# A decode step of attention and gated MLP: wo loaded behind the last V, V as the moving operand of PV, gate/up summed c-major, and wq loaded in two partition blocks

## The chip, the cores and the metric

One core of one Trainium2 chip. The metric is the device time of one execution in microseconds (us), lower is better. Each experiment is timed beside runs of the kernel before on the same chip. A "ratio" is the mean time of one kernel's fast runs over the mean of the other's fast runs of the same rounds, so it is not quite the ratio of the medians that are quoted. The profile shows one execution. Its span is about 2 us shorter than the time.

Names used by the profile: PE is the matmul engine and PEld its weight loads, DVE, ACT and POOL are the vector, scalar and GpSimd engines, SP is the engine that issues most loads. A load "lands" when its completion is signalled. SBUF is the memory on the chip that the loads write; its tiles span up to 128 partitions on the page (128x4096). The "granted clock" is the share of full speed that PE was allowed. PV is the product of the softmax weights p with V. In gate and up, m counts the 14 blocks of output columns (13 of 128, the last of 64) and c the 5 blocks of 128 input rows: "m-major" finishes one m before the next, "c-major" one c.

## The reference, cut to what matters

```python
# x: 1 token of 640; 32 heads of 128; K and V caches 32 x 4096 x 128, bf16
h  = x + attention(layernorm(x), k_cache, v_cache, wq, wo)
h2 = h + (gelu(ln(h) @ w_gate) * (ln(h) @ w_up)) @ w_down      # 640 -> 1728 -> 640
# attention: q = ln(x) @ wq; p = softmax(q . k / sqrt(128)); o = p @ v; o @ wo
```

K and V are 64 MiB (16 loads of 4 MiB, four heads each), wq and wo 5 MiB each, the MLP weights 6.3 MiB. Every byte is used once, so this is a kernel of loads.

## The kernel before

All large loads go through one queue (SP), in the order wq, K0, K1, V0, K2, V1, ..., K7, V6, wo (part), V7, wo (rest), w_gate, w_up, w_down. Three slots of SBUF hold K and V. Scores are made by a DVE product, an identity matmul that folds it, and a DVE sum. The parts that the argument touches:

```python
# wq: two column blocks, each over all 128 partitions
wq_v = A_wq[:, :].rearrange("(p c) n -> p c n", c=5)
d_wq = [P.dma("sync", wq_sb[:, 0:2, :], wq_v[:, 0:2, :]),
        P.dma("sync", wq_sb[:, 2:5, :], wq_v[:, 2:5, :])]
...
# before the last V: wo's first half and half of the second
if n == len(order) - 1:
    wo_load("0", 0, 0, 16)
    wo_load("1a", 1, 0, 8)
...
# PV: V is the weight (128 columns), p moves (4 columns); 128 of these for each group of heads
i = e.matmul(po[:, o:o + 4], vt[:, g, :], p_bd[:, G % 2, g, :], start=(g == 0), stop=(g == 127))
...
# gate and up: m-major, columns 13 apart (w_down's rows are blocked to match)
for m in range(14):
    for c in range(5):
        ws = w[:, c, m:1664:13] if m < 13 else w[:, c, 1664:1728]
        i = e.matmul(ps[0:k, m:m + 1], ws, hlnT[:, c:c + 1], start=(c == 0), stop=(c == 4))
```

The softmax here doesn't subtract the row's maximum and nothing guards it: scores larger than these inputs give would overflow.

## Time and profile before

208.41 us, median of 4 runs (208.35 to 208.57).

| of the profile before | us |
|---|---|
| span | 206.4 |
| first product of K0 starts (K0 has landed) | 25.7 |
| last V has landed | 182.9 |
| gate and up, 140 matmuls | 192.6 to 201.4 |
| last load (w_down) has landed | 202.1 |
| last matmul ends | 204.1 |

No compute engine is busy for even two thirds of the span, and the DMA row is 9 nearly throughout, so the loads set the pace.

The end of the chain of waits of the kernel before (start us, duration us, what):

```profile
182.96 1.88 PE bank L287 x64
...
192.57 8.81 PE bank L377 x140
201.38 0.64 PE bank L386 x8
202.02 2.09 PE bank L405 x37
204.11 0.02 issue
204.14 0.31 DVE out_row L412
```

From the landing of the last V on, the chain is compute: PV (L287), a projection and a layernorm (left out), gate and up (L377), the residual, w_down's product (L405).

### The profile page before, as it was taken

The page shows a single profiled execution, that of the slowest core. Times are in us where ns is not written, and L with a number is a line of the kernel's source. Part 1 is how long each engine was busy: PE and PEld are TensorE (multiplying, and loading weights), DVE is VectorE, ACT ScalarE, POOL GpSimd, SP SyncE. Part 2 cuts the span into 40 slices and gives each one's busy share as a digit, 9 for nine tenths or more (in the row PEclk, how much of TensorE's full clock was granted, in tenths as well). Part 3 has the DMA queues.
Part 4 walks back from the last instruction along what each step waited for, and adds up shares of the span by engine and source line. Part 5 has one row for each costly group of instructions (what it writes and reads, how often), then busy time and mean ns, then how long its engine had stood idle before and what let it go on. Part 6 is the DMA issues. An engine that isn't in the chain of part 4 may idle for free.

```text
span 206.4 us, 3919 instructions
## 1 busy us (share of the span) xinstructions
PE 128.2 (62%) x1715; PEld 75.2 (36%) x1715; DVE 100.3 (49%) x103; ACT 56.4 (27%) x265; POOL 3.8 (2%) x10
## 2 busy tenths in 40 slices
PE   1205058486987909671877488469818596348795
PEld 1101023132722703260327124423613186337693
DVE  3001088779479247816772877079437920000221
ACT  3001004606606602540353036205600560000101
POOL 7000000000000000000000000000000000000000
PEclk9999658969958967995797579757976985555555
DMA  6999999999999999999999999999999999999970
GB/s 219 445 448 419 464 438 407 426 467 427 413 403 470 432 416 407 470 429 419 402 470 422 426 403 465 426 422 407 464 429 426 413 403 433 421 435 429 372 285 6
DMA packets 3844, 84.47 MB, mean 409 GB/s; under 512 B 434, under 2 KB 500, under 8 KB 628
## 3 DMA queue, kind: packets, MB, share of 16 engines
q1 hardware_dynamic: 3826, 84.23, 95.8%
q8 instruction: 13, 0.21, 0.4%
q14 instruction: 3, 0.02, 0.0%
q10 hardware_dynamic: 2, 0.00, 0.0%
HBM read 84.23 MB, written 0.00 MB: 408 GB/s over the span
## 4 chain that ended last, share of the span: by engine, by line
DMA 57%; PE 24%; DVE 15%; issue 2%; SPq 1%; ACT 0%; DVEq 0%
DMA slot<-in_A_k_cache_dram 41%; DMA slot<-in_A_v_cache_dram 16%; DVE prod L251 12%; PE bank L259 10%; PE bank L287 6%; PE bank L377 4%; DVE sc L266 2%; PE bank L319 2%; PE bank L405 1%; SPq L51 1%; PE bank L386 0%; PE bank L215 0%; PE bank L298 0%; PE bank L310 0%; DVEq L419 0%
## 5 line engine op out<-in xcount | busy, mean ns | idle before, releaser
L259 PE MATMUL bank<-prod,id_b 128*128 128x512 bf16 x256 | 75.2, 454 | 50.7 <-DVE prod L251 50.7
L251 DVE TENSOR_TENSOR prod<-slot,qb 128x4096 bf16<-128x4096 bf16 x32 | 72.4, 2285 | 28.5 <-DMA slot<-in_A_k_cache_dram 28.5
L270 ACT ACTIVATE p_bd<-sc,zero_t 32x32 bf16<-32x32 f32 x128 | 46.4, 362 | 97.2 <-DVE sc L266 96.0
L259 PEld LDWEIGHTS bank<-prod,id_b 128*128 128x128 bf16 x256 | 26.9, 113 | 96.9 <-DVE prod L251 60.5
L266 DVE TENSOR_REDUCE sc<-bank 128x32 f32<-128x512 f32 x32 | 22.0, 688 | 22.3 <-PE bank L259 22.3
L287 PE MATMUL bank<-p_bd,slot 128*128 128x4 bf16 x1024 | 27.5, 165 | 6.3 <-DMA slot<-in_A_v_cache_dram 6.3
L287 PEld LDWEIGHTS bank<-p_bd,slot 128*128 128x128 bf16 x1024 | 27.4, 98 | 7.9 <-DMA slot<-in_A_v_cache_dram 3.3
L270 ACT ACTIVATION_READ_ACCUMULATOR p_bd<-sc,zero_t 32x1 f32 x128 | 23.5, 184 | 0.0
L235 PE MATMUL bank<-arena,xlnB 128*32 128x512 bf16 x40 | 4.6, 628 | 10.0 <-DMA arena<-in_A_wq_dram 10.0
L377 PE MATMUL bank<-hlnT,slot 128*128 128x1 bf16 (+1 forms) x140 | 8.8, 199 | 1.5 <-DVE hlnT L365 1.5
L377 PEld LDWEIGHTS bank<-hlnT,slot 128*128 128x128 bf16 (+1 forms) x140 | 8.7, 165 | 1.7 <-DVE hlnT L365 1.6
L303 DVE TENSOR_TENSOR attnN<-bank,rz 128x16 bf16<-128x16 f32 x2 | 0.3, 174 | 17.4 <-PE bank L287 17.4
L319 PE MATMUL bank<-aP,arena 128*128 128x1 bf16 x160 | 7.0, 179 | 1.6 <-issue 1.2
L319 PEld LDWEIGHTS bank<-aP,arena 128*128 128x128 bf16 x160 | 6.9, 132 | 1.8 <-issue 1.5
L219 ACT ACTIVATE ln<-ln,eps_t 128x1 f32<-128x1 f32 x2 | 0.6, 294 | 24.5 <-DVE ln L217 24.5
L241 DVE CAST qb<-bank 128x512 bf16<-128x512 f32 x1 | 0.7, 692 | 13.1 <-PE bank L235 13.1
L235 PEld LDWEIGHTS bank<-arena,xlnB 128*32 128x32 bf16 x40 | 1.3, 133 | 12.5 <-issue 6.3
L242 ACT CAST qb<-bank 128x512 bf16<-128x512 f32 x1 | 0.6, 585 | 13.6 <-PE bank L235 13.6
L414 ACT CAST out_row<-bank 1x160 bf16<-1x160 f32 x2 | 0.6, 285 | 6.0 <-PE bank L405 5.9
L405 PE MATMUL bank<-slot,hm 128*1 128x160 bf16 (+1 forms) x56 | 2.1, 331 | 0.0
L390 DVE COPY g_t<-bank 128x14 f32<-128x14 f32 x1 | 0.2, 173 | 3.8 <-PE bank L377 3.8
L364 DVE TENSOR_TENSOR hT<-xx,bank 128x5 f32<-128x5 f32 x1 | 0.2, 161 | 3.7 <-PE bank L319 3.7
(55 smaller groups left out, 23.1 us busy)
## 6 DMA issues: line engine op xcount, KB each, us to landing
slot<-in_A_k_cache_dram SPq DMA_DIRECT2D x8, 4096.0 KB, 22.1
slot<-in_A_v_cache_dram SPq DMA_DIRECT2D x7, 4096.0 KB, 17.5
slot<-in_A_v_cache_dram SPq DMA_DIRECT2D x2, 2048.0 KB, 29.6
arena<-in_A_wq_dram SPq DMA_DIRECT2D x1, 3072.0 KB, 14.7
arena<-in_A_wo_dram SPq DMA_DIRECT2D x1, 2560.0 KB, 23.1
arena<-in_A_wo_dram SPq DMA_DIRECT2D x2, 1280.0 KB, 30.6
slot<-in_B_w_gate_dram SPq DMA_DIRECT2D x1, 2160.0 KB, 26.5
slot<-in_B_w_up_dram SPq DMA_DIRECT2D x1, 2160.0 KB, 31.9
```

The lines of the kernel that those rows point to most:

```text
L51: ev = self.op(eng, lambda e: e.dma_start(out, in_), *deps, dma=True)
L219: l3 = A(lambda e: e.activation(ln[:, 3:4], ln[:, 2:3], ACTF.Ln, bias=eps_t[:, 0:1], scale=-1.0), l2, c_eps)
L235: i = e.matmul(ps_q[hf][32 * j:32 * j + 32, :], xlnB[:, c, :], wq_j[:, c, j, 4 * hf:4 * hf + 4, :], start=(c == 0), stop=(c == 4))
L241: qa = V(lambda e: e.tensor_copy(qb[:, 0:4, :].rearrange("p g d -> p (g d)"), ps_q[0][:, :]), qd)
L251: m = V(lambda e: e.tensor_tensor(out=prod[:, s % 4, :, :], in0=kt[:, 32 * u:32 * u + 32, :], in1=qb[:, G, :].unsqueeze(1).to_broadcast([1 ...
L259: i = e.matmul(ps_f[s % 2][:, :], id_b[:, :], prod[:, s % 4, :, 16 * b:16 * b + 16], start=(b == 0), stop=(b == 7))
L266: reds[s] = V(lambda e: e.reduce_sum(sc[:, s % 4, :], ps_f[s % 2][:, :].rearrange("p (g d) -> p g d", d=16), axis=AX.X), folds[s], exps.ge ...
L270: x = A(lambda e, j=j: e.activation(p_bd[32 * j:32 * j + 32, G % 2, 32 * (s % 4):32 * (s % 4) + 32, j], sc[32 * j:32 * j + 32, s % 4, :], ...
L287: i = e.matmul(po[:, o:o + 4], vt[:, g, :], p_bd[:, G % 2, g, :], start=(g == 0), stop=(g == 127))
L319: r = e.matmul(ps_p[:, c:c + 1], wo_sb[:, t, i, c::5], aP[:, t, i:i + 1], start=(t == 0 and c == 0 and i == 0), stop=(t == 1 and i == 15), ...
L377: i = e.matmul(ps[0:k, m:m + 1], ws, hlnT[:, c:c + 1], start=(c == 0), stop=(c == 4))
L405: i = e.matmul(ps_d[32 * q:32 * q + 1, 0:160], hm[0:k, m:m + 1], wd_sb[0:k, m, 160 * q:160 * q + 160], start=False, stop=(last and m == ms ...
```

## The change

Its intent, as we read the diff: take PV and the projection off the tail by loading all of wo behind the last V; make PV cheaper with V as the moving operand; make gate/up start on what has landed; and start the stream of loads sooner with a first load of 16 rows, one for each of the 16 DMA engines that the page counts. The diff, cut to its core:

```diff
-    wq_v = A_wq[:, :].rearrange("(p c) n -> p c n", c=5)
-    d_wq = [P.dma("sync", wq_sb[:, 0:2, :], wq_v[:, 0:2, :]),
-            P.dma("sync", wq_sb[:, 2:5, :], wq_v[:, 2:5, :])]
+    wq_v = A_wq[:, :].rearrange("(p c) n -> p (c n)", c=5)
+    d_wq = [P.dma("sync", arena[0:16, :], wq_v[0:16, :]),
+            P.dma("sync", arena[16:128, :], wq_v[16:128, :])]
 ...
-            if n == len(order) - 1:
-                wo_load("0", 0, 0, 16)
-                wo_load("1a", 1, 0, 8)
 ...   # PV: 32 matmuls for each group, p as weights of 16 columns, on four column tiles
-                    i = e.matmul(po[:, o:o + 4], vt[:, g, :], p_bd[:, G % 2, g, :], ...)
+                for b in range(32 // parts * k, 32 // parts * (k + 1)):
+                    a = 32 * (b % 4)
+                    i = e.matmul(po[a:a + 16, :], p_bd[:, G % 2, 4 * b:4 * b + 4, :].rearrange("p g j -> p (g j)"),
+                                 vt[:, 4 * b:4 * b + 4, :], start=(b < 4), stop=(b >= 28))
+        evs[G] = A(lambda e: e.copy(po_sb[:, G % 2, :], po[:, :]), pvs[G], ...)   # then 4 fp32 matmuls pick the heads
 ...
+    wo_load("0", 0, 0, 16)          # all behind the last V
+    wo_load("1a", 1, 0, 12)
+    wo_load("1b", 1, 12, 16)
 ...   # w_up in 3 + 2 of its 5 c blocks; w_down in rows 12, 13, then 8 + 2 + 2
-            for m in range(14):
-                for c in range(5):
-                    ws = w[:, c, m:1664:13] if m < 13 else w[:, c, 1664:1728]
+            for c in cs:
+                for m in range(14):
+                    ws = w[:, c, 512 * (m // 4) + m % 4:512 * (m // 4) + 512:4] if m < 12 else \
+                        w[:, c, 128 * m:min(128 * m + 128, DF)]
```

The q projection, which ran two of its five column blocks before the rest of wq had landed, now waits for both loads.

More of the change, by code (lines that the diff above doesn't have):

```diff
@@ L22 @@
 NSLOT = 3
-WD1 = 11
 class Ev:
@@ L111, in bass_sequential_preLN__gqa_block_cached__glu_gated_geglu__decode_kernel @@
     hlnT = sb("hlnT", [128, 5], BF16)
-    rz = sb("rz", [128, H], FP32)
-    attnN = sb("attnN", [128, H], BF16)
+    rz = sb("rz", [16, 2], FP32)
+    po_sb = sb("po_sb", [128, 2, 512], FP32)
+    hs_t = sb("hs_t", [128, 4, 16], FP32)
+    hs = sb("hs", [128, 4, 28], FP32)
     aT = sb("aT", [16, 2, 128], BF16)
@@ L133, in bass_sequential_preLN__gqa_block_cached__glu_gated_geglu__decode_kernel @@
     ps_g, ps_u = bank[0], bank[1]
-    ps_q = [bank[3], bank[4]]
-    ps_d = bank[3]
+    ps_q = [bank[3], bank[7]]
+    ps_a = bank[3]
+    ps_d = bank[3][:, 256:416]
     ps_o = [bank[2], bank[4]]
@@ L139, in bass_sequential_preLN__gqa_block_cached__glu_gated_geglu__decode_kernel @@
     ps_p = bank[7]
-    wq_sb = arena[:, :].rearrange("p (c n) -> p c n", c=5)
     wo_sb = arena[:, :].rearrange("p (t i n) -> p t i n", t=2, i=16)
@@ L201, in bass_sequential_preLN__gqa_block_cached__glu_gated_geglu__decode_kernel @@
                                          fill=0.0, base=0, channel_multiplier=-8), c_onesb)
+    GP(lambda e: e.memset(hs[:, :, :], 0.0))
+    c_hs = GP(lambda e: e.affine_select(hs_t[:, :, :], ones_f[:, 0:64].rearrange("p (a b) -> p a b", a=4),
+                                        pattern=[[-32, 4], [-1, 16]], compare_op=ALU.is_equal,
+                                        fill=0.0, base=0, channel_multiplier=1), c_ones)
     c_pbd = GP(lambda e: e.memset(p_bd[:, :, :, :], 0.0))
     c_rs = GP(lambda e: e.memset(RS[:, :, :], 0.0))
+    c_po = [V(lambda e, b=b: e.memset(bank[b][:, :], 0.0)) for b in (2, 4)]
+    c_hs = V(lambda e: e.reduce_sum(hs[:, :, 12:16], hs_t[:, :, :].rearrange("p t (g j) -> p g j t", g=4), axis=AX.X), c_hs)
     def x_cols(e):
@@ L228, in bass_sequential_preLN__gqa_block_cached__glu_gated_geglu__decode_kernel, with q_proj @@
     wq_j = arena[:, :].rearrange("p (c g j d) -> p c j g d", c=5, g=NG, j=4)
-    def q_part(cs):
-        def fn(e):
-            for c in cs:
-                for hf in range(2):
-                    for j in range(4):
-                        i = e.matmul(ps_q[hf][32 * j:32 * j + 32, :], xlnB[:, c, :],
-                                     wq_j[:, c, j, 4 * hf:4 * hf + 4, :], start=(c == 0), stop=(c == 4))
-            return i
-        return fn
-    T(q_part([0, 1]), xl, d_wq[0])
-    qd = T(q_part([2, 3, 4]), d_wq[1])
+    def q_proj(e):
+        for c in range(5):
+            for hf in range(2):
+                for j in range(4):
+                    i = e.matmul(ps_q[hf][32 * j:32 * j + 32, :], xlnB[:, c, :],
+                                 wq_j[:, c, j, 4 * hf:4 * hf + 4, :], start=(c == 0), stop=(c == 4))
+        return i
+    qd = T(q_proj, xl, *d_wq)
     qa = V(lambda e: e.tensor_copy(qb[:, 0:4, :].rearrange("p g d -> p (g d)"), ps_q[0][:, :]), qd)
     qc = A(lambda e: e.copy(qb[:, 4:8, :].rearrange("p g d -> p (g d)"), ps_q[1][:, :]), qd)
-    folds, reds, exps, pvs = {}, {}, {}, {}
+    folds, reds, exps, pvs, evs, hds = {}, {}, {}, {}, {}, {}
     def score_mult(s):
@@ L280, in pv_group @@
         vt = view(n)
-        po = ps_o[G // 4]
-        o = 4 * (G % 4)
+        po = ps_o[G % 2]
         parts = len(landed[n])
@@ L285, in pv @@
             def pv(e, k=k):
-                for g in range(128 // parts * k, 128 // parts * (k + 1)):
-                    i = e.matmul(po[:, o:o + 4], vt[:, g, :], p_bd[:, G % 2, g, :],
-                                 start=(g == 0), stop=(g == 127))
-                return i
-            pvs[G] = consumed[n] = T(pv, exps[4 * G + 3], landed[n][k], qc)
+                for b in range(32 // parts * k, 32 // parts * (k + 1)):
+                    a = 32 * (b % 4)
+                    i = e.matmul(po[a:a + 16, :], p_bd[:, G % 2, 4 * b:4 * b + 4, :].rearrange("p g j -> p (g j)"),
+                                 vt[:, 4 * b:4 * b + 4, :], start=(b < 4), stop=(b >= 28))
@@ new lines, in pv, with head_sum @@
+                return i
+            pvs[G] = consumed[n] = T(pv, exps[4 * G + 3], landed[n][k], evs.get(G - 2), *c_po)
+        evs[G] = A(lambda e: e.copy(po_sb[:, G % 2, :], po[:, :]), pvs[G], hds.get(G - 2))
+        def head_sum(e):
+            g = G % 4
+            for r in range(4):
+                i = e.matmul(ps_a[0:16, 128 * (G // 4):128 * (G // 4) + 128], hs[:, r, 12 - 4 * g:28 - 4 * g],
+                             po_sb[:, G % 2, 128 * r:128 * r + 128], start=(g == 0 and r == 0), stop=(g == 3 and r == 3))
+            return i
@@ L293, in bass_sequential_preLN__gqa_block_cached__glu_gated_geglu__decode_kernel @@
+        return head_sum
     zs = {}
     def sum_half(t):
-        hs = slice(16 * t, 16 * t + 16)
-        r = V(lambda e: e.reduce_sum(RT[:, hs], RS[:, hs, :], axis=AX.X), exps[16 * t + 15])
-        z = T(lambda e: e.matmul(ps_z[:, 0:16], ones_f[:, :], RT[:, hs], start=True, stop=True), r)
-        zs[t] = V(lambda e: e.reciprocal(rz[:, hs], ps_z[:, 0:16]), z)
+        hh = slice(16 * t, 16 * t + 16)
+        r = V(lambda e: e.reduce_sum(RT[:, hh], RS[:, hh, :], axis=AX.X), exps[16 * t + 15])
@@ L301, in finish_half @@
+        z = T(lambda e: e.matmul(ps_z[0:16, 0:1], RT[:, hh], ones_f[:, 0:1], start=True, stop=True), r)
+        zs[t] = V(lambda e: e.reciprocal(rz[:, t:t + 1], ps_z[0:16, 0:1]), z)
     def finish_half(t):
-        hs = slice(16 * t, 16 * t + 16)
-        z2 = V(lambda e: e.tensor_mul(attnN[:, hs], ps_o[t][:, 0:16], rz[:, hs]), zs[t], pvs[4 * t + 3])
-        ps_t = ps_z[0:16, 64:128].bitcast(BF16)
-        z3 = T(lambda e: e.transpose(ps_t, attnN[:, hs], id_b[:, :]), z2)
-        z4 = V(lambda e: e.tensor_copy(aT[:, t, :], ps_t), z3)
+        z4 = V(lambda e: e.tensor_scalar(aT[:, t, :], ps_a[0:16, 128 * t:128 * t + 128], rz[:, t:t + 1], None, ALU.mult),
+               zs[t], hds[4 * t + 3])
@@ L313, in finish_half, with proj_part @@
         return V(lambda e: e.tensor_copy(aP[:, t, :], ps_z[:, 32:48]), z5)
-    def proj_half(t, ev, *ws):
+    def proj_part(t, lo, hi, *ws):
         def fn(e):
             for c in range(5):
-                for i in range(16):
+                for i in range(lo, hi):
                     r = e.matmul(ps_p[:, c:c + 1], wo_sb[:, t, i, c::5], aP[:, t, i:i + 1],
@@ L322, in fn @@
             return r
-        return T(fn, ev, *ws)
+        return T(fn, *ws)
     def scores(G):
@@ L333, in bass_sequential_preLN__gqa_block_cached__glu_gated_geglu__decode_kernel @@
     scores(0)
+    heads = None
     for G in range(NG):
@@ L336, in bass_sequential_preLN__gqa_block_cached__glu_gated_geglu__decode_kernel @@
             scores(G + 1)
-        if G == 3:
-            sum_half(0)
-        if G == NG - 1:
-            sum_half(1)
-            proj_half(0, a0, d_wo["0"])
-        pv_group(G)
-        issue(pos[("V", G)] + 1 + NSLOT)
-        if G == 3:
-            a0 = finish_half(0)
-    wo_load("1b", 1, 8, 16)
-    sl = [slots[(len(order) + i) % NSLOT] for i in range(2)]
+        if G in (3, NG - 1):
+            sum_half(G // 4)
+        if heads is not None:
+            hds[G - 1] = T(heads, evs[G - 1], c_hs, qa, qc)
@@ L350, in bass_sequential_preLN__gqa_block_cached__glu_gated_geglu__decode_kernel @@
+        if G == 4:
+            a0 = finish_half(0)
+        heads = pv_group(G)
+        issue(pos[("V", G)] + 1 + NSLOT)
+    hds[NG - 1] = T(heads, evs[NG - 1])
+    a1 = finish_half(1)
+    wo_load("0", 0, 0, 16)
+    wo_load("1a", 1, 0, 12)
+    wo_load("1b", 1, 12, 16)
+    sl = [slots[(len(order) + i) % NSLOT] for i in range(1, 3)]
+    free = [consumed[len(order) - NSLOT + i] for i in range(1, 3)]
     wg_sb = sl[0][:, 0:5 * DF].rearrange("p (c n) -> p c n", c=5)
     wu_sb = sl[0][:, 5 * DF:10 * DF].rearrange("p (c n) -> p c n", c=5)
-    wd_sb = sl[1][:, 0:14 * D].rearrange("p (c n) -> p c n", c=14)
@@ L353, in bass_sequential_preLN__gqa_block_cached__glu_gated_geglu__decode_kernel @@
-    wd_v = B_w_down[0:1664, :].rearrange("(p c) n -> p c n", c=13)
-    d_wg = P.dma("sync", wg_sb, B_w_gate[:, :].rearrange("(p c) n -> p c n", c=5), consumed[len(order) - NSLOT])
-    d_wu = P.dma("sync", wu_sb, B_w_up[:, :].rearrange("(p c) n -> p c n", c=5))
-    d_wd = [P.dma("sync", wd_sb[0:64, 13, :], B_w_down[1664:1728, :], consumed[len(order) - NSLOT + 1]),
-            P.dma("sync", wd_sb[:, 0:WD1, :], wd_v[:, 0:WD1, :]),
-            P.dma("sync", wd_sb[:, WD1:13, :], wd_v[:, WD1:13, :])]
+    wd_sb = sl[1][:, 0:14 * D].rearrange("p (m n) -> p m n", m=14)
@@ new lines, in bass_sequential_preLN__gqa_block_cached__glu_gated_geglu__decode_kernel @@
+    wu_v = B_w_up[:, :].rearrange("(p c) n -> p c n", c=5)
+    wd_v = B_w_down[0:1536, :].rearrange("(a p r) n -> p a r n", a=3, r=4)
+    wd_d = wd_sb[:, 0:12, :].rearrange("p (a r) n -> p a r n", a=3)
+    d_wd = [P.dma("sync", wd_sb[:, 12, :], B_w_down[1536:1664, :], free[1]),
+            P.dma("sync", wd_sb[0:64, 13, :], B_w_down[1664:1728, :])]
+    d_wg = P.dma("sync", wg_sb, B_w_gate[:, :].rearrange("(p c) n -> p c n", c=5), free[0])
+    d_wu = [P.dma("sync", wu_sb[:, 0:3, :], wu_v[:, 0:3, :]),
+            P.dma("sync", wu_sb[:, 3:5, :], wu_v[:, 3:5, :])]
@@ L360, in bass_sequential_preLN__gqa_block_cached__glu_gated_geglu__decode_kernel @@
+    d_wd += [P.dma("sync", wd_d[:, 0:2, :, :], wd_v[:, 0:2, :, :]),
+             P.dma("sync", wd_d[:, 2, 0:2, :], wd_v[:, 2, 0:2, :]),
+             P.dma("sync", wd_d[:, 2, 2:4, :], wd_v[:, 2, 2:4, :])]
     V(lambda e: e.memset(ps_g[64:128, 13:14], 0.0), reds[31])
     V(lambda e: e.memset(ps_u[64:128, 13:14], 0.0), reds[31])
-    a1 = finish_half(1)
-    pr = proj_half(1, a1, d_wo["1a"], d_wo["1b"])
+    proj_part(0, 0, 16, a0, d_wo["0"])
+    proj_part(1, 0, 12, a1, d_wo["1a"])
+    pr = proj_part(1, 12, 16, d_wo["1b"])
@@ L368, in bass_sequential_preLN__gqa_block_cached__glu_gated_geglu__decode_kernel, with glu @@
                                      in1=hT[:, 0:5].unsqueeze(1).to_broadcast([128, 128, 5]), op=ALU.mult), h, c_idf)
-    def glu(ps, w):
+    def glu(ps, w, cs):
         def fn(e):
-            for m in range(14):
-                k = 128 if m < 13 else 64
-                for c in range(5):
-                    ws = w[:, c, m:1664:13] if m < 13 else w[:, c, 1664:1728]
-                    i = e.matmul(ps[0:k, m:m + 1], ws, hlnT[:, c:c + 1], start=(c == 0), stop=(c == 4))
-            return i
-        return fn
-    ga = T(glu(ps_g, wg_sb), hl, d_wg)
-    up = T(glu(ps_u, wu_sb), d_wu)
+            for c in cs:
+                for m in range(14):
+                    ws = w[:, c, 512 * (m // 4) + m % 4:512 * (m // 4) + 512:4] if m < 12 else \
+                        w[:, c, 128 * m:min(128 * m + 128, DF)]
+                    k = 128 if m < 13 else 64
+                    i = e.matmul(ps[0:k, m:m + 1], ws, hlnT[:, c:c + 1], start=(c == 0 and m == 0), stop=(c == 4),
+                                 skip_group_check=True)
+            return i
+        return fn
+    ga = T(glu(ps_g, wg_sb, range(5)), hl, d_wg)
     def resid(e):
@@ L388, in resid @@
         return i
-    T(resid, hx, qa)
+    T(resid, hx)
+    T(glu(ps_u, wu_sb, range(3)), d_wu[0])
+    up = T(glu(ps_u, wu_sb, range(3, 5)), d_wu[1])
     g1 = V(lambda e: e.tensor_copy(g_t[:, :], ps_g[:, 0:14]), ga)
@@ L409, in down @@
         return fn
-    T(down([13] + list(range(WD1)), False), g9, d_wd[0], d_wd[1])
-    dn = T(down(list(range(WD1, 13)), True), d_wd[2])
+    T(down([12, 13], False), g9, d_wd[0], d_wd[1])
+    T(down(range(8), False), d_wd[2])
+    T(down([8, 9], False), d_wd[3])
+    dn = T(down([10, 11], True), d_wd[4])
     os = [V(lambda e, q=q: e.tensor_copy(out_row[0:1, 160 * q:160 * q + 160], ps_d[32 * q:32 * q + 1, 0:160]), dn)
```

## The prediction

The forecast came to 206.4 us, 2.0 below the 208.41 before: 1.7 from the tail, which leaves 0.3 for the start (how the start was weighed is not stated). The start was also on the critical path, with a gain of up to 0.5 us from a shorter ramp, and a possible loss by the 16-partition load. "This cost" is that loss. What stays of it is the range: its top, 209.3, allowed a net loss of 0.9 us against before. Cut too is a rule for the column step; the 30 to 40 ns for a step of 4 lie between the measured 29 (step 1) and 45 (step 5).

> **What bounds the kernel now.** DMA, then a PE tail. The page gives PE 62%, DVE 49%, ACT 27%, but its DMA row reads 9 from the second slice to the 38th. The stretches view shows 385 to 495 GB/s in every 2.5 us from 5 to 192 us: the queue never runs dry. 84.47 MB between 2.6 and 201.9 us is 423 GB/s. From 198.5 us the rate halves (271, 220, 230, 166, 67 GB/s): some DMA engines finish about 3 us before others. The down-projection piece issued last lands at about 202.1 (171.5 + 30.6).
>
> The chain of waits ends otherwise: last V lands 182.9, PV half 1.9, normalise/transpose/spread 1.5, proj 3.6 (80 matmuls, 45 ns each), layernorm 2.5, gate and up 8.8 (140 matmuls, 63 ns), residual 0.6, down 2.1 (56 matmuls, 37 ns) to 204.1, output 2.3, end 206.4. The tail is PE-bound by about 1.7 us over the last landing.
>
> **What the change does.**
> - V before wo: 3840 KB of wo leave the place ahead of V7, about 9.3 us at 422 GB/s; V7 lands near 173.6. PV, head sum and both projections then run under the loads. No byte is saved; the last landing does not move.
> - PV: 128 weight loads and matmuls per group (3.3 us) become 32 matmuls of 512 columns on four column tiles. The q projection has that form: 24 in 2.75 us, so about 3.7 us per group. Added: one ACT eviction (0.58 us, as q's 128x512 cast) and four fp32 head-sum matmuls per group. PE and ACT had slack there: worth about 0.
> - Gate/up: the column step goes from 13 to 4 elements. [...] 29 ns per last-V matmul (step 1), 45 (step 5), 63 (step 13), all at clock 0.50. I expect 30 to 40 ns. In c-major order most of up runs before its last rows land. The activations should be ready near 198.5, before the down rows.
> - Then the tail is: last down piece lands 202, 8 matmuls 0.3, output 2.3: span 204.6, gain 1.7 us.
> - wq as 16 + 112 partitions: the first DMA has one row per engine, so the ramp (mostly under 330 GB/s from 2.2 to 3.8 us) may shorten by up to 0.5 us. [...] I give this cost four chances in ten, mostly partial.
>
> **On the critical path:** only the tail (-1.7 us)[...].
>
> **Prediction:** 206.4 us, range 204.3 to 209.3; faster by over 2%: 0.11, within 2%: 0.84, slower by over 2%: 0.05.
>
> **Shown right by:** a chain that ends with w_down's DMA, not gate/up; last byte near 202; gate/up at 30 to 40 ns; DMA still 9s. The first K landing (25.7 before) shows the start: under 25.5 a faster ramp[...].
>
> **Made wrong by:**[...] step 4 no faster than 13 (gain 0.3 us); PV freeing V slots late; or the DMA engines' finish spread shrinking, which could give 2 us more.

## More of the kernel before

The head of the page, four of its rows of 40 time slices and queues, for the kernel before (busy tenths for DMA, then GB/s in each slice; then packets, MB and share of a queue):

```profile
span 206.4 us, 3919 instructions
PE 128.2 (62%) x1715; PEld 75.2 (36%) x1715; DVE 100.3 (49%) x103; ACT 56.4 (27%) x265; POOL 3.8 (2%) x10
...
DMA  6999999999999999999999999999999999999970
GB/s 219 445 448 419 464 438 407 426 467 427 413 403 470 432 416 407 470 429 419 402 470 422 426 403 465 426 422 407 464 429 426 413 403 433 421 435 429 372 285 6
...
q8 instruction: 13, 0.21, 0.4%
```

## The result, and the profile after

218.0 us, median of 4 runs (217.74 to 218.46), against 208.41 (208.35 to 208.57). Ratio 1.0461, 95% interval 1.0443 to 1.048: slower by 4.6%, about 9.6 us.

The same rows of the page for the kernel after:

```profile
span 216.2 us, 2508 instructions
PE 121.3 (56%) x1009; PEld 58.8 (27%) x1009; DVE 100.8 (47%) x104; ACT 61.1 (28%) x273; POOL 4.1 (2%) x12
...
DMA  9999899999999999999999999999999999999992
GB/s 121 227 250 242 220 436 436 424 443 406 464 396 394 449 418 452 418 436 432 430 430 430 436 415 455 414 430 430 436 430 433 415 418 433 424 405 394 406 403 76
...
q8 instruction: 8, 0.13, 0.3%
```

The DMA row reads 9 or 8 from the first slice (before: 6, then 9). But "busy" is not "moving": the GB/s row stands at 220 to 250 in slices 2 to 5, where before it stood at 419 to 464. The loss sits in the first 27 us. (The busy share is the time that packets took, and here they took longer: in the trace a 40 KB packet took 5.1 us in the median in the first wq load and 2.8 us in the second, and 1.51 us in a_wq_one below.)

The issue tables, loads of wq alone, before and then after (size, then median us from issue to landing):

```profile
arena<-in_A_wq_dram SPq DMA_DIRECT2D x1, 3072.0 KB, 14.7
arena<-in_A_wq_dram SPq DMA_DIRECT2D x1, 2048.0 KB, 7.8
```

```profile
arena<-in_A_wq_dram SPq DMA_DIRECT2D x1, 4480.0 KB, 26.7
arena<-in_A_wq_dram SPq DMA_DIRECT2D x1, 640.0 KB, 8.5
```

The same 5120 KB landed 12 us later (27.9 for 15.9). The timelines show what that delays, first of the kernel before, then of the kernel after (start us, duration us, engine, line, operation; in brackets the idle time and what ended it):

```profile
15.98 2.75 PE L235 MATMUL bank<-arena,xlnB 128*32 128x512 bf16 x24 [5.29 <-DMA arena<-in_A_wq_dram]
25.67 4.49 DVE L251 TENSOR_TENSOR prod<-slot,qb 128x4096 bf16<-128x4096 bf16 x2 [6.20 <-DMA slot<-in_A_k_cache_dram]
```

```profile
28.07 4.46 PE L240 MATMUL bank<-arena,xlnB 128*32 128x512 bf16 x40 [22.99 <-DMA arena<-in_A_wq_dram]
37.67 4.49 DVE L254 TENSOR_TENSOR prod<-slot,qb 128x4096 bf16<-128x4096 bf16 x2 [4.40 <-DMA slot<-in_A_k_cache_dram]
```

The first K product starts at 37.67 instead of 25.67, 12.0 us later. From there to the end is 216.2 - 37.7 = 178.5 us after and 206.4 - 25.7 = 180.7 us before: the rest of the change gained 2.2 us, which the start gave away more than five times over. The end of the chain after the change:

```profile
189.26 22.68 DMA slot<-in_B_w_down_dram
211.94 0.04 issue
211.98 1.50 PE bank L429 x40
213.48 0.04 issue
213.53 0.46 PE bank L429 x8
213.99 0.02 issue
214.01 0.31 DVE out_row L438
```

It now ends in a load, as foretold: eight matmuls follow the last landing instead of gate/up and all of w_down.

### The profile page after: what moved, and what is told of

Its sections match the earlier page's. It is cut to its first block, busy times and chain, and to the rows that moved or that the text cites. A ratio compares the mean times of both kernels' runs of the same rounds, so it can differ in the third digit from the quotient of the medians.

```text
span 216.2 us, 2508 instructions
## 1 busy us (share of the span) xinstructions
PE 121.3 (56%) x1009; PEld 58.8 (27%) x1009; DVE 100.8 (47%) x104; ACT 61.1 (28%) x273; POOL 4.1 (2%) x12
## 4 chain that ended last, share of the span: by engine, by line
DMA 67%; DVE 14%; PE 13%; issue 3%; SPq 2%; DVEq 0%
DMA slot<-in_A_k_cache_dram 46%; DVE prod L254 12%; DMA slot<-in_A_v_cache_dram 11%; DMA slot<-in_B_w_down_dram 10%; PE bank L262 8%; PE bank L291 3%; DVE sc L269 2%; SPq L51 2%; PE bank L300 1%; PE bank L429 1%; DVEq L445 0%; DVE out_row L438 0%; PE bank L311 0%; DVE RT L310 0%
## 5 line engine op out<-in xcount | busy, mean ns | idle before, releaser
L291 PE MATMUL bank<-slot,p_bd 128*16 128x512 bf16 x256 | 17.3, 380 | 0.4 <-DMA slot<-in_A_v_cache_dram 0.4
L291 PEld LDWEIGHTS bank<-slot,p_bd 128*16 128x16 bf16 x256 | 9.4, 89 | 4.6 <-DMA slot<-in_A_v_cache_dram 0.9
L300 PE MATMUL bank<-po_sb,hs 128*16 128x128 f32 x64 | 8.4, 274 | 1.1 <-ACT po_sb L295 1.1
L399 PE MATMUL bank<-hlnT,slot 128*128 128x1 bf16 (+1 forms) x140 | 6.7, 176 | 3.5 <-DMA slot<-in_B_w_gate_dram 3.5
L399 PEld LDWEIGHTS bank<-hlnT,slot 128*128 128x128 bf16 (+1 forms) x140 | 6.3, 118 | 4.4 <-issue 4.1
L295 ACT COPY po_sb<-bank 128x512 f32<-128x512 f32 x8 | 4.7, 585 | 7.4 <-PE bank L291 7.4
L300 PEld LDWEIGHTS bank<-po_sb,hs 128*16 128x16 f32 x64 | 5.5, 96 | 4.5 <-issue 2.1
L315 DVE TENSOR_SCALAR aT<-bank,rz 16x128 bf16<-16x128 f32 x2 | 0.7, 340 | 5.8 <-PE bank L300 5.8
```

Source lines behind the costliest of these rows:

```text
L291: i = e.matmul(po[a:a + 16, :], p_bd[:, G % 2, 4 * b:4 * b + 4, :].rearrange("p g j -> p (g j)"), vt[:, 4 * b:4 * b + 4, :], start=(b < 4) ...
L295: evs[G] = A(lambda e: e.copy(po_sb[:, G % 2, :], po[:, :]), pvs[G], hds.get(G - 2))
L300: i = e.matmul(ps_a[0:16, 128 * (G // 4):128 * (G // 4) + 128], hs[:, r, 12 - 4 * g:28 - 4 * g], po_sb[:, G % 2, 128 * r:128 * r + 128], s ...
```

## The experiments

Fifteen runs, two of them repeats of a kernel; all gave correct results.

### A. Is it the loads of wq, or the rest?

Theory: the split of wq into partitions 0-15 and 16-127 carries the loss. Rival: PV, head sums or load order cost the time. A second rival: full rows of 40 KB are slow whatever their partitions. Three kernels here and a_wq_mid of part B, 3 rounds each, in one call (one visit to a chip).

**a_wq_old**: the kernel after, with wq as before.

```diff
-            P.dma("sync", arena[0:16, :], wq_v[0:16, :]), P.dma("sync", arena[16:128, :], wq_v[16:128, :])
+            P.dma("sync", wq_sb[:, 0:2, :], wq_v[:, 0:2, :]), P.dma("sync", wq_sb[:, 2:5, :], wq_v[:, 2:5, :])
```

> The kernel after, with only the two wq loads put back to two column blocks over all 128 partitions. Theory[...]: wq lands near 16 us and K0 near 25.7 instead of 27.9 and 37.6; the whole run falls by about 12 us, to a span of 204 and about 206 us, so slightly faster than before. Rival (the new PV, head sums or load order cost the 10 us): K0 lands at 25.7 but the time stays above 212.

Measured: 205.75 us, ratio 0.9895 (0.9867 to 0.9922), span 205.1 (the profiled run was the slowest of its four). K0 landed at 25.3 us, 23.6 us after its issue.

**b_wq_16**: the kernel before, with only the 16 + 112 loads, and the q projection waiting for both.

> The kernel before, with only wq loaded as partitions 0 to 15 and then 16 to 127 in full 40 KB rows, and the q projection waiting for both. Theory: K0 lands near 37.6 and the time rises by 11 to 12 us, to about 220. Rival (the loss belongs to the other changes): within 1 us of before.

Measured: 220.63 us, ratio 1.0599 (1.0576 to 1.0623); first K product at 38.14 us. One edit made alone carries the whole loss, and undone it takes the whole loss away. The rival of "the rest" falls.

**a_wq_one**: the kernel after, with wq as one load.

```diff
-    d_wq = [P.dma("sync", arena[0:16, :], wq_v[0:16, :]), P.dma("sync", arena[16:128, :], wq_v[16:128, :])]
+    d_wq = [P.dma("sync", arena[:, :], wq_v[:, :])]
```

> The kernel after, with wq as one load of 128 partitions in full 40 KB rows. [...] wq lands near 16 us, K0 near 25.7, about 206 us. Rival (40 KB rows are slow by themselves): K0 lands well after 28 and the time stays near 218.

Measured: 205.61 us, ratio 0.9872 (0.9855 to 0.9888), span 204.2, first K product at 25.78. Rows of 40 KB are not slow. This version beats both kernels by a change of one line. The first K product in the timelines of b_wq_16 and then of a_wq_one:

```profile
38.14 4.49 DVE L250 TENSOR_TENSOR prod<-slot,qb 128x4096 bf16<-128x4096 bf16 x2 [4.73 <-DMA slot<-in_A_k_cache_dram]
```

```profile
25.78 4.49 DVE L253 TENSOR_TENSOR prod<-slot,qb 128x4096 bf16<-128x4096 bf16 x2 [4.39 <-DMA slot<-in_A_k_cache_dram]
```

### B. Which partitions, or how many?

If the number of partitions decides, two loads of 64 are slow alike; if it is which partitions, they can differ. The author expected the second: 32-95 at full rate, the blocks 0-31, 96-127, 0-63 and 64-127 slow.

**a_wq_mid**: wq as 32-95, then 0-31, then 96-127.

```diff
+    d_wq = [P.dma("sync", arena[32:96, :], wq_v[32:96, :]),
+            P.dma("sync", arena[0:32, :], wq_v[0:32, :]),
+            P.dma("sync", arena[96:128, :], wq_v[96:128, :])]
```

> The kernel after, with wq as partitions 32 to 95, then 0 to 31, then 96 to 127, full rows. [...] Rival (any load of fewer than 128 partitions is slow in the same measure): the first load takes about 12 us.

**a_wq_64**: wq as 0-63, then 64-127. It was run at another time.

> The kernel after with wq as partitions 0 to 63 and then 64 to 127, full rows. [...] 2560 KB take 12.0 us where the 64 partitions 32 to 95 took about 7; the first piece lands near 15.5, both by 27.5, K0 near 37; about 217. Rival (fewer than 128 partitions, whichever): the first half lands at 10.7 as 32 to 95 did.

The issue tables of a_wq_mid and then of a_wq_64, loads of wq (of two loads the median stands):

```profile
arena<-in_A_wq_dram SPq DMA_DIRECT2D x1, 2560.0 KB, 9.9
arena<-in_A_wq_dram SPq DMA_DIRECT2D x2, 1280.0 KB, 18.0
```

```profile
arena<-in_A_wq_dram SPq DMA_DIRECT2D x2, 2560.0 KB, 21.6
```

The first load has the same size and the same number of partitions (64) in both, and was issued at 0.8 us. It landed at 10.7 us in a_wq_mid and at 16.4 us in a_wq_64. So the number of partitions does not decide; which partitions does. The packets show how. Each row is one packet of 40 KB, and its median time in the trace was 1.51 us in a_wq_one and in the first load of a_wq_mid (27 GB/s), 3.1 us in the two quarters of a_wq_mid and 3.20 us in a_wq_64: twice as long. In the kernel after, the 16 packets of the first load, partitions 0-15, took from 1.8 to 7.9 us together, 5.1 us each in the median. (The same rows of wq always go to the same partitions, so the side that reads is not ruled out separately. What makes some partitions slow is not shown.) Landings in us:

| wq loaded as | pieces | K0 | time |
|---|---|---|---|
| 128, columns 2 + 3 (before) | 8.7, 15.9 | 25.6 | 208.41 |
| 128, one load | 16.1 | 25.8 | 205.61 |
| 32-95, 0-31, 96-127 | 10.7, 16.9, 22.7 | 32.4 | 212.61 |
| 16 + 112 (after) | 9.3, 27.9 | 37.6 | 218.0 |
| 64 + 64 | 16.4, 29.0 | 38.6 | 218.95 |

The last three rows and the second are one kernel but for the shape of this load (ratios to before: 0.9872, 1.0214, 1.0461, 1.0497; 64 + 64 ran in 1 round, two runs). The two quarters of a_wq_mid took about 6 us each for 1280 KB (16.9 - 10.7 and 22.7 - 16.9), which makes about 12 us for a half of 2560 KB, the figure expected for a_wq_64; its landings and K0 came within 1.6 us of what was expected. In the kernel after, the second load hurts more than the first: 27.9 - 9.3 = 18.6 us between the landings for 4480 KB, 246 GB/s, where the same bytes at the 432 GB/s of the kernel before's second load (3072 KB in 7.28 us) would need 10.6 us: 8 us lost. The first load's packets took 6.1 us for 640 KB, 108 GB/s, where the same rate would need 1.5: some 4.5 us lost.

Why the second load was quite so slow is not shown. In the trace the first packet of K0 starts at 25.4 us and the last of wq ends at 27.4, so 97 of the 112 rows were complete before any packet of K0 began.

### C. What was the rest of the change worth?

The reference from here is the kernel after with wq as one load. Five rounds each; one_mmajor and one_out have three. They were run at other times.

**one_again**: the reference itself.

> The kernel after with wq as one load, run again as the reference of this call: ratio 0.987 to before, span 204.2, last landing about 201.4, so the chain ends in the loads of w_down.

Measured: ratio 0.990 (0.9887 to 0.9913); the same code had 0.9872 on the earlier chip run, so differences between calls of 0.3% mean nothing here.

**b_vfirst**: the kernel before, with only all of wo (16, 8 and 8 rows) behind the last V and projected after it.

> The kernel before, with only all of wo loaded behind the last V and projected after it. Theory (order takes PV, spread and projection off the tail, and gate/up at 63 ns then end it): V7 lands near 173.6 instead of 182.9; span about 205.3, 1 us less than before, ratio 0.995. Rival (order alone gives the full 2.2 us): ratio 0.988 to 0.990, chain ending in a load.

Measured: ratio 1.0007 (0.9995 to 1.002): worth nothing, and both theories missed. V7 landed near 173.5 (the second half of PV, which waits for it, began at 173.48), but the second projection half waits for the last 8 rows of wo (landed 186.5), takes 3.3 us, and with the layernorm gate/up starts at 192.45 instead of 192.57. Then up waits for its own landing at 197.3 and takes 4.4 us.

**one_glu13**: the reference with gate, up and w_down as before (step 13, m-major, w_down in 11 + 2 rows).

> The same, with gate, up and w_down as in the kernel before (column step 13, m-major, 11 + 2 row pieces). Theory (gate/up at 63 ns would again end after the last landing): matmuls from gate's landing near 191.1 take 8.8 us, then 0.6 residual, 0.4 and 2.1 down: end about 206, 1.5 to 2 us more than the reference. Rival (the tail is set by the last landing alone, and the gate/up form is worth nothing): within 0.4 us of the reference.

Measured: ratio 0.9947 (0.9934 to 0.996), span 205.3 against 204.0. The size is below what was expected and the reason differs: up ended at 200.0, and then all 56 matmuls of w_down waited for the 1760 KB piece, which landed at 200.8:

```profile
200.91 2.13 PE L420 MATMUL bank<-slot,hm 64*1 64x160 bf16 x56 [0.94 <-DMA slot<-in_B_w_down_dram]
```

In the reference only 8 matmuls were left when the last piece had landed. So with the large piece the speed of gate/up did not matter: the chain went through the load. With the small pieces it would: up done at 200.0 instead of 198.8, then 0.33 us and w_down's 2.13 us, would end at about 202.4 for 201.8 (an estimate from these two traces). The two were not undone one at a time, so how the gain divides is not shown.

**one_c1** and **one_mmajor** test why gate/up took 48 ns a matmul on average, not the 30 to 40 foretold. one_c1 reads contiguous columns (w_down then comes in rows of 1280 bytes); one_mmajor keeps the step of 4 and goes back to m-major order:

```diff
 one_c1:
-                    ws = w[:, c, 512 * (m // 4) + m % 4:512 * (m // 4) + 512:4] if m < 12 else ...
+                    ws = w[:, c, 128 * m:min(128 * m + 128, DF)]
 one_mmajor:
-            for c in cs:
-                for m in range(14):
+            for m in range(14):
+                for c in range(5):
```

> The reference of this call with gate, up and w_down in plain 128-row blocks, so that each weight load reads 128 contiguous columns; still c-major. Theory (the step of 4 columns costs, 48 ns measured): about 29 ns a matmul, as in the last V of before. Rival (c-major order costs, not the step): stays near 48 ns. w_down then comes in 1280-byte rows, which may move the last landing by up to 1 us; if not, the span stays within 0.5 us of the reference, since a load ends it.

> The kernel after with wq as one load and gate/up in m-major order, still with the step of 4, up in one go behind both of its pieces. If the step sets the time of a weight load: about 48 ns a matmul, as c-major. If c-major order costs: 30 to 40 ns. End: up can start only at about 197, takes 3.4, then 0.4 and 2.1 down: about 205.2, up to 1 us more than c-major.

The timelines, gate only, of the kernel after, one_c1 and one_mmajor in turn, all at a granted clock of 0.50:

```profile
203.70 3.35 PE L399 MATMUL bank<-hlnT,slot 128*128 128x1 bf16 x70 [3.50 <-DMA slot<-in_B_w_gate_dram]
```

```profile
191.61 2.95 PE L396 MATMUL bank<-hlnT,slot 128*128 128x1 bf16 x70 [3.44 <-DMA slot<-in_B_w_gate_dram]
```

```profile
191.30 2.54 PE L398 MATMUL bank<-hlnT,slot 128*128 128x1 bf16 x70 [3.59 <-DMA slot<-in_B_w_gate_dram]
```

| order, column step | ns a matmul (us / 70, or 8.81 / 140) |
|---|---|
| m-major, 13 (before) | 63 |
| c-major, 4 (after) | 48 |
| c-major, 1 (one_c1) | 42 |
| m-major, 4 (one_mmajor) | 36 |

The averages suggest that the order costs 12 ns a matmul and the last bit of step 6 ns. The starts of the single matmuls in the trace say something else. The last of the 14 blocks, m = 13, has only 64 columns; c-major comes to it five times in gate, m-major once. Away from it, the median from one start to the next is this, for matmuls of 128 columns:

| order, column step | ns from start to start |
|---|---|
| m-major, 13 (before) | 60 |
| c-major, 4 (after) | 33 |
| c-major, 1 (one_c1) | 27 |
| m-major, 4 (one_mmajor) | 32 |

At equal step the order costs nothing (33 and 32). Around each 64-column matmul of c-major the three gaps are about 95, 143 and 55 ns, some 190 ns more than three gaps of 33; five of these instead of one group are the difference between 3.35 and 2.54 us. The view by shape agrees, for gate and up together, first of the kernel after, then of one_mmajor (busy us, then mean ns):

```profile
L399 PE MATMUL bank<-hlnT,slot 128*64 128x1 bf16 x10 | 2.1, 213 | 0.0
```

```profile
L398 PE MATMUL bank<-hlnT,slot 128*64 128x1 bf16 x10 | 0.8, 196 | 0.0
```

So the theory of one_c1 (about 29 ns) and the 30 to 40 ns of one_mmajor were both right for the 128-column matmuls, and its rival "order" was right about the average alone. Why the narrow block costs that much is open. For the time it hardly matters: one_c1 had ratio 0.991 (0.9897 to 0.9922) beside one_again's 0.990, and one_mmajor 0.9872 (0.9856 to 0.9887), for the chain ends near the loads in all of them. one_mmajor's foretold loss of up to 1 us did not come.

**one_out**: the last eviction as one DVE cast of 97 partitions, four rows of which are stored, for 0.35 us less.

> The kernel after with wq as one load and the last eviction as one DVE cast of 97 partitions, from which four rows are stored, in place of two casts each on DVE and ACT. The tail after the last matmul should lose one cast (0.35 us): ratio about 0.985 to before, if the store with four rows is not slower.

Measured: ratio 0.9898 (0.9881 to 0.9914), no gain: the reference had 0.990 and 0.9872, and one_mmajor, another form of gate/up, 0.9872. The casts did shrink from 0.66 us for two to 0.33 for one, but the issue of the store with four rows took 0.64 us instead of 0.31.

### D. The new PV is off the chain. Is it worth nothing?

**b_vfirst2**: b_vfirst with wq as one load, wo in 16 + 12 + 4 rows and the residual before up. It differs from one_glu13 in PV's form (and the order of two small loads).

> The kernel before with wq as one load, all of wo behind the last V in pieces of 16, 12 and 4 rows projected as they land, and the residual before up; PV, gate, up and w_down as before. It differs from the earlier run with old gate/up (ratio 0.9947, span 205.3) in the form of PV with its head sums, and in the order of two small loads. Theory (PV's form is off the critical path and worth nothing): ratio 0.993 to 0.997, span 205.0 to 205.6. Rival (the new PV is what gained there): ratio 0.999 to 1.001, as with order alone.

Measured: ratio 0.999 (0.9972 to 1.0007), against 0.9947 (0.9934 to 0.996) for one_glu13. It was run at another time. The theory that PV's form is worth nothing fell; the rival's number came. Yet PV is early in both: the projection after it waits for wo, not for PV. What differs is when loads land: V7 at 173.8 and 172.4, w_up at 197.2 and 195.5, both kernels moving the same weights.

The trace holds 16 completions for every large load here, and the page counts 16 DMA engines. We take the first and the last completion as a measure of how far the engines have drifted apart; the traces do not name the engine of a completion. In the kernel before, the mean busy share of the engines fell from 0.96 (197 to 198 us) to 0.12 (201 to 202 us), so some were idle while others still worked. For the load that landed last:

| kernel | instructions | 16 KB instruction packets | first completion | last completion | ratio |
|---|---|---|---|---|---|
| before | 3919 | 13 | 199.0 | 202.1 | 1 |
| b_vfirst2 | 3918 | 13 | 198.8 | 202.4 | 0.999 |
| one_glu13 | 2504 | 8 | 198.9 | 201.5 | 0.9947 |
| one_again | 2507 | 8 | 199.2 | 201.3 | 0.990 |

The first completion comes at the same time everywhere (199.0 by 0.2 us); the last one comes earlier where there are fewer instructions. (These are single profiles, and one goes against the pattern: in a_wq_old, with 8 packets, 15 completions had come by 200.8 and the last at 202.3; that was the slowest of its four runs.) PE's old PV has 1024 weight loads and 1024 matmuls, the new one 256 and 256. The page lists a DMA queue of kind "instruction": 13 packets in the kernel before (0.21 MB, 16 KB each), which took 0.99 to 1.28 us each in its trace, between 46 and 202 us, and 8 in the kernel after (0.91 to 1.35 us each). From the one to the other, 1411 instructions fewer came with 5 packets fewer. Whether the packets hold up the engine that runs the instructions is not tested here; the question is whether they hold up the loads.

Two kernels raise the instruction count and nothing else that the tail waits for. The reference, **mm_again**, is one_mmajor again.

> The kernel after with wq as one load and gate/up m-major with step 4, run again as the reference of this call: ratio 0.987 to 0.990, last landing about 201.3, 8 instruction packets.

**mm_pv128** cuts each PV matmul into four of 128 columns; **mm_dummy** adds 115 matmuls of nothing after PV of groups 1 to 6.

```diff
 mm_pv128:
+                    for r in range(4):
+                        i = e.matmul(po[a:a + 16, 128 * r:128 * r + 128], p_bd[...same...],
+                                     vt[:, 4 * b + r, :], start=(b < 4 and r == 0), stop=(b >= 28), ...)
 mm_dummy:
+                if 1 <= G < NG - 1:
+                    for _ in range(115):
+                        e.matmul(ps_p[0:1, 480:481], one_bf[0:1, 0:1], one_bf[0:1, 0:1], start=True, stop=True)
```

> The reference, with each PV matmul cut into four of 128 columns: the same p weights, the same V moving, the same sums, but 128 weight loads and matmuls per group as in the kernel before. Theory (the old PV cost not PE time but instructions: 13 packets of 16 KB instead of 8, each about 1 us[...]): 13 or so packets, the 16 completions of the last w_down load spread over 3 us instead of 2.1, last landing near 202.2, 0.6 to 1 us more time, ratio 0.992 to 0.995. Rival (it is V as weight against V moving, or PE time): ratio as the reference's within 0.15%.

> The reference, with 115 one-column matmuls of nothing after PV of groups 1 to 6: 1380 instructions more, which no result needs; PE has slack there. Theory: as with the cut matmuls, 13 or so instruction packets, last landing near 202.2, 0.6 to 1 us more. Rival: no change, as nothing in the tail waits for them.

The PE line and the instruction queue of the page, for mm_again, mm_pv128 and mm_dummy in turn:

```profile
PE 118.3 (58%) x1009; PEld 57.2 (28%) x1009; DVE 100.7 (49%) x104; ACT 61.1 (30%) x273; POOL 4.1 (2%) x12
...
q8 instruction: 8, 0.13, 0.3%
```

```profile
PE 120.6 (59%) x1777; PEld 64.5 (31%) x1777; DVE 100.8 (49%) x104; ACT 61.1 (30%) x273; POOL 4.1 (2%) x12
...
q8 instruction: 14, 0.23, 0.4%
```

```profile
PE 136.2 (66%) x1699; PEld 75.3 (37%) x1699; DVE 100.7 (49%) x104; ACT 61.1 (30%) x273; POOL 4.1 (2%) x12
...
q8 instruction: 13, 0.21, 0.4%
```

| kernel | packets | first completion of the last load | last completion | ratio (95%) |
|---|---|---|---|---|
| mm_again | 8 | 199.2 | 201.6 | 0.9882 (0.9862 to 0.9902) |
| mm_dummy | 13 | 199.1 | 202.5 | 0.9928 (0.991 to 0.9947) |
| mm_pv128 | 14 | 199.3 | 202.7 | 0.9956 (0.9942 to 0.997) |

mm_pv128 keeps V moving and loses 0.7%; mm_dummy computes nothing of use and loses 0.5%. PE's busy time does not order them: it grew by 2.3 us in the first and by 17.9 us in the second. Nor were the loads issued late: the last V was issued at 150.8 us in mm_again and 150.7 in mm_dummy, yet landed at 173.1 and 173.8. In both kernels the first completion comes as before and the last one 0.9 and 1.1 us later. So it is the number of instructions, not the form of PV, that moves the landings. That the packets do it, by holding some engine back, fits the counts (8, 13 and 14); the profile does not say which engine moved which packet, so that link is inferred, not shown. mm_pv128's extra 0.3% over mm_dummy, just outside what was expected, is not explained.

## Why the prediction was wrong, point by point

- **The failed step: "wq as 16 + 112 partitions".** The cost named there was a real one (the packets of partitions 0-15 took 5.1 us for 1.51), and b_wq_16 and a_wq_old show that the split of wq is where the time went. But the slip was 12.0 us. The sum took the first load alone, and that is the smaller part: 6.1 us for 640 KB instead of 1.5 at 432 GB/s. The term that failed is the second load, of 112 partitions, which the sum left out as if it ran at full rate: 18.6 us between the landings (246 GB/s) instead of about 10.6, so some 8 of the 12 us. The trace of the kernel before has no large load of fewer than 128 partitions, so neither figure could be read from it. Why the second load was that slow stays open.
- **"Four chances in ten, mostly partial"**: this cost was discounted, and the prediction gives no reason for it. The range allowed a net loss of 0.9 us; the start alone gave away 12.0 (first K product at 37.67 for 25.67). The hoped-for shorter ramp did not show: the first slice moved at 121 GB/s, before at 219.
- **The tail: span 204.6 without the slip, gain 1.7 us.** Right: spans of 204.0 to 205.1 with wq put back or in one load, a gain of 2.2 us after the first K product; the chain ends in w_down's load; V7 lands near 173.6 (172.4 to 173.8 measured without the slip); last landing 201.3 to 202.3 for 202.
- **But not for the reasons given,** so that the number came out is partly luck. "V before wo" alone was worth nothing (1.0007). PV was "worth about 0" and is worth about 0.4% (0.999 against 0.9947), by part D through its number of instructions. A third part comes from the small last pieces of w_down together with the faster gate/up (0.9947 against 0.990).
- **PV at 3.7 us a group**: about 2.2 us (17.3 us busy for the eight groups of the kernel after), over-estimated, off the chain.
- **Gate/up at 30 to 40 ns**: 33 ns from start to start for the 128-column matmuls, so the step was judged right; 48 ns on average, for the five interruptions by the 64-column block, which were not considered.
- **"the DMA engines' finish spread shrinking, which could give 2 us more"** named the spread without a cause. It was 3.1 us before and 2.1 us in one_again; part D ties it to the number of instructions, which the change cut.

The version to keep is the kernel after with wq in one load: 205.61 us, ratio 0.9872 and 0.990, so 1.0 to 1.3% faster than before.

## What to carry to other kernels

Load full 128-partition tiles, and when a load must be cut, cut it along columns (two column blocks cost nothing here: 205.75 us against 205.61), and try a cut along partitions before it is trusted: a 40 KB packet took 1.51 us to partitions 32-95 as to all 128, about 3.1 us to 0-31 and 96-127, 3.20 us in the halves 0-63 and 64-127, and 5.1 us to 0-15. One bad load at the head of an otherwise saturated queue delays everything behind it by its whole loss (12.0 us at K0 here). Read a DMA row of busy tenths together with its GB/s: the busy share here was 9 at half the rate. In a kernel bound by loads, count instructions as well: 1380 useless ones cost 0.5% here, and the last landing came later while the first completion came as before. Before an average over matmuls is explained, look at the single ones: one odd shape can carry it.
